# The chunk decay of units six to nine: two small DMAs from the last token's row instead of matmuls with a column of ones

## The chip, the cores and the metric

One core of one Trainium2 chip. The metric is device time in microseconds (us) of one execution, less being better; of the kernel before there are three timed runs, with a median of 182.37 us (182.37 to 183.64). One further execution was profiled; its trace is the source of all durations below.

## The reference

A gated linear attention runs over 768 tokens for 4 batches of 8 heads with 48 channels, and its output, laid out as 3072 tokens by 384 channels, goes through a two-layer perceptron with 2048 hidden units.

```python
f = 1.0 / (1.0 + np.exp(-f_logit))
for t in range(S):
    state = f[:, :, t, :, None] * state + np.einsum('bhd,bhe->bhde', k[:, :, t], v[:, :, t])
    y[:, :, t] = np.einsum('bhd,bhde->bhe', q[:, :, t], state)
...
h = x @ w_in
g = np.maximum(0.01 * h, h)
return (g @ w_out).astype(np.float32)
```

Inputs and output are float32.

## The kernel before

**Tiling.** The tokens are cut into six chunks of 128. A unit j is one chunk c of two batches, so there are twelve units, in the order c = 0 to 5 and, inside a chunk, two pairs of batches h. The half a (0 or 1) of a unit is one of its two batches. Tokens lie on the 128 partitions when data come in. With a running sum of log-decays inside a chunk, the recurrence becomes three matmul products per chunk (scores, masked scores by values, queries by the carried state), and a state that is carried from chunk to chunk.

**Steps of a unit, by their names in the order string.** `Lf`, `Lk`, `Lq`, `Lv` load a half of f, k, q, v (192 KB each, L100). `gate` (ScalarE, L140 and L141) turns f into lf = log(1 + exp(-f)), which is minus the log of the decay. `cs` (TensorE) sums lf over the tokens with an upper triangular matrix of ones (L146, 384 columns), so that row t of its PSUM tile holds the sum up to token t; row 127 is the whole chunk's. For all units but the last two (j below 10, where there is a next chunk), four more matmuls (L149) take lf itself as weights, two heads at a time, and multiply them by a column of ones: the sum over all tokens then comes out with head and channel on the partitions, four columns, in the same PSUM tile. `dec` (ScalarE) takes exponents: em and a from the 384 columns (L156, L157), and from those four columns the chunk's decay a_end (L160). `k` and `q` scale k and q; `v` casts v. For units 6 and up GpSimd does these, and `xk`, `xq` are DMA transposes on the SP queue (L203). `sc`, `mk`, `mx`, `xt` compute and copy out the unit's attention output. `pt` and `sf` compute and add the chunk's contribution to the state; `sb` (GpSimd, `state_end`) multiplies the state by a_end, a per-partition factor for each of four head pairs (L273), and casts it to bf16 (L276). `up`, `pr`, `dn`, `ob`, `st` are the perceptron: first layer (L293, L306), leaky relu on ScalarE (L299, L323), second layer (L328), copy out of PSUM, store (L341). `up` tiles go through two PSUM buffers (`ps_m`), so an `up` waits for the `pr` of the `up` two before it.

**Layout of the decay.** The state has 128 partitions: head i of a pair p has its 48 channels d at partitions 64 i to 64 i + 47, and the pair p is a column. The decay must come in that layout. In row 127 of the cs tile the same sums lie along one partition, as 384 columns (p, i, d).

**Order of the work.** All instructions are issued by one hand-written list, `order`; each engine runs its part of it in order. The SP queue issues all input loads, stores and DMA transposes, in the order of the list. Input tiles have six buffers for each of f, k, q, v, so the f tile of unit j is loaded anew by unit j + 6; for j from 6 on there is no such unit.

**Around the change.** In the list, loads run some two units ahead. The loads of unit 9's second half, for instance, follow `Lv_9_0` and stand shortly before `xq_8`; `gate_9` needs both halves of f of unit 9.

Of the kernel before, what the change touches and what calls it, by code (L numbers as in the profile page):

```python
# [9 lines left out]
FP32 = mybir.dt.float32  # L10
BF16 = mybir.dt.bfloat16
AF = mybir.ActivationFunctionType
# [3 lines left out]
def kernel(  # L16
# [10 lines left out]
    nc = tc.nc  # L27

    B, H, S, D = q.shape
    assert (B, H, S, D) == (4, 8, 768, 48)  # L30
    C = 128
    NCH = S // C
    P2 = H // 2
# [4 lines left out]
    pairs = [(c, h) for c in range(NCH) for h in range(B // 2)]  # L38
    NP = len(pairs)
    BY_UNIT = 6  # L40
    K_DVE = 6
    Q_DVE = 3
    CQ_ACT = 2

    const = ctx.enter_context(tc.tile_pool(name="const", bufs=1))
    inp = ctx.enter_context(tc.tile_pool(name="inp", bufs=6))
    work = ctx.enter_context(tc.tile_pool(name="work", bufs=2))
# [31 lines left out]
    w_in_b = [const.tile([128, NK, hi - lo], BF16, name="w_in_b", tag=f"w_in{lo}") for lo, hi in w_in_cols]  # L79
    w_out_b = const.tile([128, NF, KD], BF16, tag="w_out")  # L80

    for t in v2s:
        nc.gpsimd.memset(t[:, :, 1:3, :], 0.0)
    for t in state_b + state_f:
# [2 lines left out]
    st = {j: {} for j in range(NP)}  # L87
    srcs = {"f": f_logit, "k": k, "q": q, "v": v}

    def once(j, key, make):  # L90
        if key not in st[j]:
            st[j][key] = make()
        return st[j][key]

    def raw(j, name):
        return once(j, name + "_raw", lambda: inp.tile([128, 2, H, D], FP32, name=f"{name}_raw", tag=f"{name}_raw"))

    def load(j, name, a):
        c, h = pairs[j]
        nc.sync.dma_start(out=raw(j, name)[:, a],  # L100
                          in_=srcs[name][2 * h + a, :, c * C:(c + 1) * C, :].rearrange("h t d -> t h d"))
# [32 lines left out]
    def half(j, i):  # L134
        return slice(i, i + 1) if j < BY_UNIT else slice(0, 2)
# [7 lines left out]
    def cs(j, a):  # L143
        lf = lfs[j % NR]
        t = st[j]["cs", a] = ps_g.tile([128, 512], FP32, name="cs", tag="g")
        nc.tensor.matmul(t[:, 0:H * D], ut, lf[:, a, :, 0:D], start=True, stop=True)  # L146
        if pairs[j][0] < NCH - 1:
            for p in range(P2):
                nc.tensor.matmul(t[:, H * D + p:H * D + p + 1], lf[:, a, 2 * p:2 * p + 2, :], ones_col,  # L149
                                 start=True, stop=True)  # L150

    def dec(j, a):
        t = st[j].pop(("cs", a))
        em = once(j, "em", lambda: work.tile([128, 2, H * D], BF16, name="em_t", tag="em_t", bufs=3))
        at = once(j, "a", lambda: work.tile([128, 2, H * D], BF16, name="a_t", tag="a_t", bufs=3))
        nc.scalar.activation(em[:, a], t[:, 0:H * D], AF.Exp, scale=1.0)  # L156
        nc.scalar.activation(at[:, a], t[:, 0:H * D], AF.Exp, scale=-1.0)  # L157
        if pairs[j][0] < NCH - 1:
            end = st[j]["end", a] = work.tile([128, P2], FP32, name="a_end", tag="a_end", bufs=12)
            nc.scalar.activation(end, t[:, H * D:H * D + P2], AF.Exp, scale=-1.0)  # L160

    def scale_k(j, i):
        a = half(j, i)
# [4 lines left out]
    def scale_q(j, i):  # L168
        a = half(j, i)
        eng = nc.vector if j < Q_DVE else nc.gpsimd  # L170
        eng.tensor_mul(qhs[j % NR][:, a, :, 0:D], raw(j, "q")[:, a],  # L171
# [11 lines left out]
    def turned(j, x):  # L183
        return once(j, x + "T", lambda: work.tile([128, 2 * P2, 128], BF16, name=x + "T", tag=x + "T", bufs=3))
# [9 lines left out]
    def turn_out(j, a, x):  # L194
        out, src = turned(j, x)[:, P2 * a:P2 * a + P2, :], st[j].pop(("tp" + x, a))
        if x == "q" and j < CQ_ACT:
            nc.scalar.copy(out=out, in_=src)
# [160 lines left out]
    def store_part(j, a, i):  # L358
# [3 lines left out]

    parts = {
        "gate": gate, "cs": cs, "dec": dec, "k": scale_k, "q": scale_q, "v": cast_v,
        "tk": lambda j, a: turn(j, a, "k"), "tq": lambda j, a: turn(j, a, "q"),
        "ck": lambda j, a: turn_out(j, a, "k"), "cq": lambda j, a: turn_out(j, a, "q"),
        "xk": lambda j, a=None: turn_dma(j, "k", a), "xq": lambda j, a=None: turn_dma(j, "q", a),
        "sc": score, "mk": mask, "mx": mix, "xt": x_out, "pt": state, "sf": state_add, "sb": state_end,
        "up": up, "pr": relu, "uu": up_unit, "uh": up_half, "ph": relu_half, "pu": relu_unit, "W": weights, "H": hold, "dn": down, "ob": out_copy, "st": store,
        "dp": down_part, "op": out_part, "sp": store_part,  # L370
        "Lf": lambda j, a: load(j, "f", a), "Lk": lambda j, a: load(j, "k", a),
        "Lq": lambda j, a: load(j, "q", a), "Lv": lambda j, a: load(j, "v", a),
    }
# [27 lines left out]
    v_5_0 xt_4_1 tk_5_0 Lq_6_1 dec_5_1 dn_3_0_3 sb_3_1 dn_2_1_3 Lv_6_1 k_5_1 up_4_0 v_5_1 ob_2_1 Lf_7_0 pt_5_0 tq_5_0  # L401
    q_5_1 sf_5_0 dn_3_1_0 gate_6_0 st_2_1 up_4_1 ck_5_0 tk_5_1 Lk_7_0 dn_3_1_1 ck_5_1 pr_4_1 cq_5_0 tq_5_1 dn_3_1_2
    Lq_7_0 ob_3_0 pr_4_0 pt_5_1 Lv_7_0 cs_6_0 v_6_0 sf_5_1 dn_4_0_0 dec_6_0 cq_5_1 cs_6_1 st_3_0 up_4_2 sb_4_0 dec_6_1
    dn_3_1_3 Lf_7_1 up_4_3 pr_4_2 ob_3_1 k_6_0 Lk_7_1 sc_5_2 pr_4_3 up_4_4 st_3_1 mk_5_0_0 sb_4_1 dn_4_0_1 mk_5_1_0
    pr_4_4 xk_6 up_4_5 mk_5_0_1 q_6_0 pt_6_0 mk_5_1_1 up_4_6 pr_4_5 Lq_7_1 Lv_7_1 sf_6_0 gate_7_0 mx_5_2 up_4_7 xt_5_0
    sb_5_0 xq_6 pr_4_6 pt_6_1 xt_5_1 dn_4_0_2 pr_4_7 sf_6_1 up_5_0 Lf_8_0 cs_7_0 Lk_8_0 pr_5_0 up_5_1 dec_7_0 cs_7_1
    dn_4_0_3 Lq_8_0 up_5_2 pr_5_1 v_7_0 ob_4_0 dec_7_1 dn_4_1_0 Lv_8_0 up_5_3 sb_5_1 pr_5_2 st_4_0 dn_4_1_1 pr_5_3
    up_5_4 k_7_0 Lf_8_1 sc_6_2 pr_5_4 up_5_5 Lk_8_1 mk_6_0_1 q_7_0 dn_5_0_0 xk_7 mk_6_0_0 pr_5_5 up_5_6 mk_6_1_1
    dn_5_0_1 Lq_8_1 mk_6_1_0 pr_5_6 up_5_7 xq_7 mx_6_2 pr_5_7 gate_8_0 dn_4_1_2 Lv_8_1 xt_6_0 pt_7_0 xt_6_1 dn_5_0_2
    Lf_9_0 up_6_0 dn_5_0_3 pr_6_0 Lk_9_0 cs_8_0 ob_5_0 dn_4_1_3 dec_8_0 Lq_9_0 up_6_1 ob_4_1 cs_8_1 st_5_0 sf_7_0  # L410
    pr_6_1 up_6_2 dec_8_1 v_8_0 dn_6_0_0 st_4_1 up_6_3 pr_6_2 Lv_9_0 q_8_0 dn_5_1_0 pr_6_3 Lf_9_1 up_6_4 sc_7_2 Lk_9_1
    pr_6_4 k_8_0 up_6_5 mk_7_0_1 xq_8 dn_6_0_1 mk_7_0_0 pr_6_5 sb_6_0 up_6_6 mk_7_1_1 xk_8 dn_6_0_2 mk_7_1_0 pr_6_6
    sb_6_1 up_6_7 Lq_9_1 mx_7_2 pr_6_7 Lv_9_1 gate_9_0 dn_6_0_3 xt_7_0 sb_7_0 pt_7_1 pt_8_0 ob_6_0 dn_5_1_1 Lf_10_0
    sf_8_0 cs_9_0 dn_5_1_2 st_6_0 xt_7_1 dec_9_0 dn_6_1_0 sf_7_1 Lk_10_0 dn_5_1_3 dn_6_1_1 Lq_10_0 sc_8_2 Lv_10_0
    v_9_0 dn_6_1_2 mk_8_1_0 up_7_0 Lf_10_1 mk_8_1_1 sb_7_1 ob_5_1 up_7_1 pr_7_0 Lk_10_1 mk_8_0_1 dn_6_1_3 pr_7_1
    mk_8_0_0 st_5_1 up_7_2 cs_9_1 Lq_10_1 pr_7_2 up_7_3 dec_9_1 mx_8_2 Lv_10_1 up_7_4 pr_7_3 k_9_0 Lf_11_0 xt_8_0
    dn_7_0_0 xt_8_1 pr_7_4 Lk_11_0 ob_6_1 up_7_5 gate_10_0 sb_8_0 pt_9_0 xk_9 up_8_0 pt_9_1 q_9_0 dn_7_0_1 pr_7_5
    sf_9_1 st_6_1 pt_8_1 pr_8_0 cs_10_0 up_7_6 Lq_11_0 sf_8_1 dec_10_0 v_10_0 up_8_1 sf_9_0 pr_7_6 dn_7_0_2 xq_9
    sb_8_1 pr_8_1 cs_10_1 up_7_7 dec_10_1 up_8_2 Lv_11_0 Lf_11_1 pr_7_7 q_10_0 dn_8_0_0 pr_8_2 up_8_3 dn_7_0_3 Lk_11_1
    pr_8_3 k_10_0 up_8_4 ob_7_0 xq_10 dn_8_0_1 pr_8_4 dn_7_1_0 xk_10 up_8_5 sc_9_2 pr_8_5 st_7_0 up_8_6 mk_9_0_1  # L420
    gate_11_0 Lq_11_1 dn_7_1_1 mk_9_0_0 up_8_7 mk_9_1_0 pr_8_6 dn_7_1_2 mk_9_1_1 Lv_11_1 pr_8_7 dn_8_0_2 cs_11_0
    mx_9_2 dec_11_0 cs_11_1 xt_9_0 dn_7_1_3 dec_11_1 xt_9_1 dn_8_0_3 ob_7_1 k_11_0 up_9_0 ob_8_0 st_7_1 sc_10_2 pr_9_0
    st_8_0 dn_8_1_0 mk_10_1_0 q_11_0 xk_11 up_9_1 mk_10_0_0 dn_8_1_1 mk_10_1_1 pr_9_1 sb_9_0 up_9_2 xq_11 mk_10_0_1
    dn_9_0_0 pr_9_2 sb_9_1 up_9_3 mx_10_2 pr_9_3 v_11_0 up_9_4 xt_10_0 dn_9_0_1 xt_10_1 pr_9_4 up_9_5 up_10_0 pr_9_5
    sc_11_2 pr_10_0 up_10_1 mk_11_1_0 up_9_6 mk_11_0_0 pr_10_1 dn_9_0_2 mk_11_0_1 pr_9_6 up_10_2 mk_11_1_1 up_9_7
    pr_10_2 mx_11_2 pr_9_7 up_10_3 xt_11_0 dn_9_0_3 xt_11_1 pr_10_3 up_10_4 ob_9_0 up_11_0 st_9_0 pr_10_4 dn_8_1_2
    pr_11_0 up_10_5 up_11_1 pr_10_5 dn_8_1_3 pr_11_1 up_10_6 ob_8_1 up_11_2 st_8_1 pr_10_6 dn_9_1_0 pr_11_2 up_10_7
    up_11_3 pr_10_7 dn_9_1_1 pr_11_3 up_11_4 dn_9_1_2 pr_11_4 up_11_5 dn_9_1_3 pr_11_5 up_11_6 ob_9_1 dn_11_0_0
    st_9_1_2 pr_11_6 up_11_7 dn_10_0_0 pr_11_7 dn_11_0_1 dn_10_0_1 dn_11_0_2 dn_10_0_2 dn_11_0_3 dn_10_0_3 ob_11_0
    st_11_0_2 dn_11_1_0 ob_10_0 st_10_0 dn_11_1_1 dn_11_1_2 dn_11_1_3 dp_10_1_0 ob_11_1 st_11_1 op_10_1_0 sp_10_1_0  # L430
    dp_10_1_1 op_10_1_1 sp_10_1_1
    """
    for word in order.split():
        name, *numbers = word.split("_")
# [31 lines left out]
```

## Time and profile before

| | |
|---|---|
| Timed runs | 182.37, 183.64, 182.37 us |
| Profiled execution | 183.06 us, span on the core 181.3 us |
| TensorE busy | 168.4 us, 93% of the span |
| ScalarE, VectorE, GpSimd busy | 101.3, 88.1, 76.3 us |
| Matmuls of L149 | 80, of them 32 in units 6 to 9 (79.5 to 120.6 us) |
| a_end (L160) | 20 instructions, median 180 ns |
| Input loads | 96 of 192 KB, median 3.7 to 3.9 us from issue to landing |
| HBM traffic | 25.17 MB read, 4.72 MB written |

Starts are counted from the start of the span. [...] A load's row on the SP queue is the time that the queue takes to issue it, not its flight. The DMA share is the mean busy share of 16 DMA engines; it was 0.95 to 1.06 in every stretch from 20 to 147 us.

### The profile page before, as it was taken

Reading aid. Unit: us, or ns where it says so; the run is one execution under the profiler, and the core shown is the slowest. Engines: PE = TensorE matmul, PEld = TensorE weight load, DVE = VectorE, ACT = ScalarE, POOL = GpSimd, SP = SyncE. Lnnn points to the kernel's source line nnn. Section 1 sums busy time; section 2 is a strip of 40 time slices with the busy share of each in tenths; the row PEclk is TensorE's granted clock in tenths of the full one; section 3 lists DMA queues with packets and bytes.
Section 4 is the critical chain, followed back from the end, with each engine's and each line's share of the span. In section 5 each row is a group of like instructions: output and inputs, shape, how many; then the busy total and the mean of one; then the engine's idle time right before and its main releaser. Section 6 shows DMA issues by size and latency. Waiting matters only on the chain.

```text
span 181.3 us, 5431 instructions
## 1 busy us (share of the span) xinstructions
PE 168.4 (93%) x2264; PEld 131.4 (72%) x2264; DVE 88.1 (49%) x184; ACT 101.3 (56%) x207; POOL 76.3 (42%) x139
## 2 busy tenths in 40 slices
PE   0467999999999999999999999999999999999993
PEld 0245789776778888778877777688876788887663
DVE  2369750047778778657426425555135725311031
ACT  4475447456565757395865666268757346465100
POOL 8229900044754730939493186329730940000000
PEclk9999999999999999999999999999999999999999
DMA  6999999999998997899998999999996730110122
GB/s 121 194 217 192 188 209 215 193 186 251 200 214 173 213 219 156 169 228 254 161 240 165 213 214 189 209 231 187 219 172 161 120 88 4 43 47 0 43 87 87
DMA packets 118736, 30.23 MB, mean 167 GB/s; under 512 B 113080, under 2 KB 117944, under 8 KB 118712
## 3 DMA queue, kind: packets, MB, share of 16 engines
q1 hardware_dynamic: 116408, 26.75, 72.6%
q0 software_dynamic: 2304, 3.15, 10.1%
q8 instruction: 17, 0.28, 0.6%
q14 instruction: 7, 0.06, 0.1%
HBM read 25.17 MB, written 4.72 MB: 165 GB/s over the span
## 4 chain that ended last, share of the span: by engine, by line
PE 89%; SPq 6%; DMA 2%; ACT 1%; issue 0%; DVE 0%
PE po L328 34%; PE pm L293 24%; PE pm L306 12%; PE py L252 6%; SPq L100 6%; PE pw L219 4%; PE tp L192 3%; PE cs L146 2%; DMA f_raw<-in_f_logit_dram 2%; PE pt L263 2%; PE po L350 1%; PE pm L313 1%; PE cs L149 1%; ACT e_t L140 0%; ACT lf L141 0%
## 5 line engine op out<-in xcount | busy, mean ns | idle before, releaser
L328 PE MATMUL po<-w_out_b,gT 128*128 128x384 bf16 x368 | 71.6, 326 | 0.0
L299 ACT ACTIVATE gT<-pm 128x512 bf16<-128x512 f32 x64 | 37.8, 599 | 32.7 <-PE pm L293 32.3
L293 PE MATMUL pm<-xT,w_in_b 128*128 128x256 bf16 x384 | 51.0, 273 | 0.0
L328 PEld LDWEIGHTS <-gT 128*128 128x128 bf16 x368 | 33.8, 98 | 16.0 <-issue 0.2
L293 PEld LDWEIGHTS <-w_in_b 128*128 128x128 bf16 x384 | 40.0, 110 | 6.3
L224 DVE TENSOR_TENSOR wm<-pw,ut 128x512 bf16<-128x512 f32 x48 | 30.5, 684 | 17.6 <-PE pw L219 17.4
L333 DVE COPY osb<-po 128x384 f32<-128x384 f32 x23 | 12.8, 555 | 40.8 <-PE po L328 40.4
L178 POOL CAST v_b<-v_raw 128x384 bf16<-128x384 f32 (+1 forms) x18 | 11.1, 617 | 41.2 <-DMA v_raw<-in_v_dram 31.9
L323 ACT ACTIVATE gT<-pm 128x512 bf16<-128x512 f32 x30 | 17.9, 598 | 12.7 <-PE pm L306 11.9
L306 PE MATMUL pm<-xT,w_in_b 128*128 128x128 bf16 x360 | 24.2, 219 | 0.0
L306 PEld LDWEIGHTS <-w_in_b 128*128 128x128 bf16 x360 | 21.9, 110 | 1.7
L258 DVE CAST xT<-py 128x384 bf16<-128x384 f32 x24 | 12.7, 554 | 16.8 <-PE py L252 16.7
L171 POOL TENSOR_TENSOR qh<-q_raw,a_t 128x384 bf16<-128x384 f32 (+1 forms) x12 | 15.4, 1283 | 11.3 <-issue 6.0
L156 ACT ACTIVATE em_t<-cs 128x384 bf16<-128x384 f32 x24 | 11.8, 492 | 9.7 <-PE cs L149 8.0
L276 POOL CAST sb<-sf 64x192 bf16<-64x192 f32 x40 | 14.7, 367 | 2.5
L140 ACT ACTIVATE e_t<-f_raw 128x384 f32<-128x384 f32 (+1 forms) x18 | 11.3, 628 | 7.7 <-DMA f_raw<-in_f_logit_dram 7.7
L146 PE MATMUL cs<-lf,ut 128*128 128x384 bf16 x24 | 8.5, 353 | 6.7 <-ACT lf L141 6.7
L165 POOL TENSOR_TENSOR kh<-k_raw,em_t 128x768 bf16<-128x768 f32 x6 | 9.9, 1648 | 10.8 <-ACT em_t L156 7.4
L157 ACT ACTIVATE a_t<-cs 128x384 bf16<-128x384 f32 x24 | 11.8, 490 | 0.0
L141 ACT ACTIVATE lf<-e_t 128x384 bf16<-128x384 f32 (+1 forms) x18 | 11.3, 630 | 0.6
L273 POOL TENSOR_TENSOR sf<-sf,a_end 128x192 f32<-128x192 f32 x20 | 10.5, 524 | 2.2 <-DVE sf L269 1.8
L149 PEld LDWEIGHTS <-lf 128*128 128x128 bf16 x80 | 5.2, 100 | 7.6 <-issue 6.2
(51 smaller groups left out, 159.8 us busy)
## 6 DMA issues: line engine op xcount, KB each, us to landing
f_raw<-in_f_logit_dram SPq DMA_DIRECT2D x24, 192.0 KB, 3.9
k_raw<-in_k_dram SPq DMA_DIRECT2D x24, 192.0 KB, 3.8
q_raw<-in_q_dram SPq DMA_DIRECT2D x24, 192.0 KB, 3.7
v_raw<-in_v_dram SPq DMA_DIRECT2D x24, 192.0 KB, 3.7
out_dram<-osb SPq DMA_DIRECT2D x21, 192.0 KB, 3.0
w_out_b<-in_moe_w_out_dram POOLq DMA_DIRECT2D x4, 384.0 KB, 11.1
w_in_b<-in_moe_w_in_dram POOLq DMA_DIRECT2D x1, 768.0 KB, 10.0
w_in_b<-in_moe_w_in_dram POOLq DMA_DIRECT2D x2, 192.0 KB, 4.9
```

What stands on the lines that cost most here:

```text
L146: nc.tensor.matmul(t[:, 0:H * D], ut, lf[:, a, :, 0:D], start=True, stop=True)
L156: nc.scalar.activation(em[:, a], t[:, 0:H * D], AF.Exp, scale=1.0)
L171: eng.tensor_mul(qhs[j % NR][:, a, :, 0:D], raw(j, "q")[:, a], st[j]["a"][:, a].rearrange("t a (h d) -> t a h d", d=D))
L224: nc.vector.tensor_mul(wm, st[j].pop(("pw", a, i)), ut[:, None, :].to_broadcast([128, P2, 128]))
L258: nc.vector.tensor_copy(out=xT[:, :, a, :], in_=st[j].pop(("py", a))[:, 0:NK, :])
L276: nc.gpsimd.tensor_copy(out=sb[rows, a, :, i * D:i * D + D], in_=sf[rows, a])
L293: nc.tensor.matmul(pm[:, i, :], w_in(kk, ff), st[j]["xT"][:, kk].rearrange("t a s -> t (a s)"), start=(kk == 0), stop=(kk == NK - 1))
L299: nc.scalar.activation(gT[:, 2 * g:2 * g + 2, :], st[j].pop(("pm", g)), AF.Prelu, alpha=0.01)
L306: nc.tensor.matmul(pm[:, i, :], w_in(kk, ff), st[j]["xT"][:, kk, a, :], start=(kk == 0), stop=(kk == NK - 1))
L323: nc.scalar.activation(gT[:, 4 * g:4 * g + 4, 128 * a:128 * a + 128], st[j].pop(("pu", a, g)), AF.Prelu, alpha=0.01)
L328: nc.tensor.matmul(po, st[j]["g"][:, ff, 128 * a:128 * a + 128], w_out_b[:, ff, :], start=(ff == 0), stop=(ff == NF - 1))
L333: nc.vector.tensor_copy(out=osb, in_=st[j].pop(("po", a)))
```

## The change

For units 6 to 9 the 32 matmuls of L149 and the small exponent of L160 are taken out. In their place `dec` takes the exponent of the last 32 rows (partitions 96 to 127) of the cs tile, all 384 columns, and writes it as float32 into the unit's f tile, which is no longer needed; the columns are reordered as (i, d, a, p), so that the four p of one channel are neighbours (16 bytes) and the next channel stands 32 bytes further. Only row 127 is used; the two halves interleave in the tile. A new step `xe` then issues two DMAs on the SP queue, one for each head i: 1,536 bytes of partition 127 go to 48 partitions, 32 bytes each, in one of four constant tiles `end`, which GpSimd fills with ones at the start. `state_end` reads that tile. The step `xe_6` stands in the list after `Lk_7_1`, `xe_7` between `st_4_0` and `Lf_8_1`, `xe_8` between `Lv_9_0` and `Lf_9_1`, and `xe_9` between `Lf_11_0` and `Lk_11_0` of the SP queue's order. The rest of the list is the same.

```diff
+    END_DMA = 6
...
+    ends = [const.tile([128, 2, P2], FP32, name=f"end{i}", tag=f"end{i}") for i in range(4)]
+    for t in ends:
+        nc.gpsimd.memset(t, 1.0)
...
-        if pairs[j][0] < NCH - 1:
+        if pairs[j][0] < NCH - 1 and j < END_DMA:
             for p in range(P2):
                 nc.tensor.matmul(t[:, H * D + p:H * D + p + 1], lf[:, a, 2 * p:2 * p + 2, :], ones_col,
                                  start=True, stop=True)
...
         if pairs[j][0] < NCH - 1:
-            end = st[j]["end", a] = work.tile([128, P2], FP32, name="a_end", tag="a_end", bufs=12)
-            nc.scalar.activation(end, t[:, H * D:H * D + P2], AF.Exp, scale=-1.0)
+            if END_DMA <= j:
+
+                last = last_row(j)[96:128, :, :, a, :].rearrange("t i d p -> t p i d")
+                nc.scalar.activation(last, t[96:128, 0:H * D].rearrange("t (p i d) -> t p i d", p=P2, i=2), AF.Exp, scale=-1.0)
+                st[j]["end", a] = ends[j % 4][:, a]
+            else:
+                end = st[j]["end", a] = work.tile([128, P2], FP32, name="a_end", tag="a_end", bufs=12)
+                nc.scalar.activation(end, t[:, H * D:H * D + P2], AF.Exp, scale=-1.0)
+
+    def last_row(j):
+        return raw(j, "f").rearrange("t a h d -> t (a h d)").rearrange("t (i d a p) -> t i d a p", i=2, d=D, a=2)
+
+    def end_out(j):
+        last = raw(j, "f").rearrange("t a h d -> t (a h d)")[127:128]
+        for i in range(2):
+            nc.sync.dma_start(out=ends[j % 4][64 * i:64 * i + D].rearrange("d a p -> d (a p)"),
+                              in_=last[:, i * D * 2 * P2:(i + 1) * D * 2 * P2])
...
+        "xe": end_out,
```

More of the change, by code (lines that the diff above doesn't have):

```diff
@@ L369 @@
         "up": up, "pr": relu, "uu": up_unit, "uh": up_half, "ph": relu_half, "pu": relu_unit, "W": weights, "H": hold, "dn": down, "ob": out_copy, "st": store,
-        "dp": down_part, "op": out_part, "sp": store_part,
+        "xe": end_out, "dp": down_part, "op": out_part, "sp": store_part,
         "Lf": lambda j, a: load(j, "f", a), "Lk": lambda j, a: load(j, "k", a),
@@ L403 @@
     Lq_7_0 ob_3_0 pr_4_0 pt_5_1 Lv_7_0 cs_6_0 v_6_0 sf_5_1 dn_4_0_0 dec_6_0 cq_5_1 cs_6_1 st_3_0 up_4_2 sb_4_0 dec_6_1
[L404 to L431, printed above, removed]
+    dn_3_1_3 Lf_7_1 up_4_3 pr_4_2 ob_3_1 k_6_0 Lk_7_1 xe_6 sc_5_2 pr_4_3 up_4_4 st_3_1 mk_5_0_0 sb_4_1 dn_4_0_1
+    mk_5_1_0 pr_4_4 xk_6 up_4_5 mk_5_0_1 q_6_0 pt_6_0 mk_5_1_1 up_4_6 pr_4_5 Lq_7_1 Lv_7_1 sf_6_0 gate_7_0 mx_5_2
@@ new lines @@
+    up_4_7 xt_5_0 sb_5_0 xq_6 pr_4_6 pt_6_1 xt_5_1 dn_4_0_2 pr_4_7 sf_6_1 up_5_0 Lf_8_0 cs_7_0 Lk_8_0 pr_5_0 up_5_1
+    dec_7_0 cs_7_1 dn_4_0_3 Lq_8_0 up_5_2 pr_5_1 v_7_0 ob_4_0 dec_7_1 dn_4_1_0 Lv_8_0 up_5_3 sb_5_1 pr_5_2 st_4_0
+    dn_4_1_1 xe_7 pr_5_3 up_5_4 k_7_0 Lf_8_1 sc_6_2 pr_5_4 up_5_5 Lk_8_1 mk_6_0_1 q_7_0 dn_5_0_0 xk_7 mk_6_0_0 pr_5_5
+    up_5_6 mk_6_1_1 dn_5_0_1 Lq_8_1 mk_6_1_0 pr_5_6 up_5_7 xq_7 mx_6_2 pr_5_7 gate_8_0 dn_4_1_2 Lv_8_1 xt_6_0 pt_7_0
+    xt_6_1 dn_5_0_2 Lf_9_0 up_6_0 dn_5_0_3 pr_6_0 Lk_9_0 cs_8_0 ob_5_0 dn_4_1_3 dec_8_0 Lq_9_0 up_6_1 ob_4_1 cs_8_1
@@ new lines @@
+    st_5_0 sf_7_0 pr_6_1 up_6_2 dec_8_1 v_8_0 dn_6_0_0 st_4_1 up_6_3 pr_6_2 Lv_9_0 q_8_0 xe_8 dn_5_1_0 pr_6_3 Lf_9_1
+    up_6_4 sc_7_2 Lk_9_1 pr_6_4 k_8_0 up_6_5 mk_7_0_1 xq_8 dn_6_0_1 mk_7_0_0 pr_6_5 sb_6_0 up_6_6 mk_7_1_1 xk_8
+    dn_6_0_2 mk_7_1_0 pr_6_6 sb_6_1 up_6_7 Lq_9_1 mx_7_2 pr_6_7 Lv_9_1 gate_9_0 dn_6_0_3 xt_7_0 sb_7_0 pt_7_1 pt_8_0
+    ob_6_0 dn_5_1_1 Lf_10_0 sf_8_0 cs_9_0 dn_5_1_2 st_6_0 xt_7_1 dec_9_0 dn_6_1_0 sf_7_1 Lk_10_0 dn_5_1_3 dn_6_1_1
+    Lq_10_0 sc_8_2 Lv_10_0 v_9_0 dn_6_1_2 mk_8_1_0 up_7_0 Lf_10_1 mk_8_1_1 sb_7_1 ob_5_1 up_7_1 pr_7_0 Lk_10_1
@@ new lines @@
+    mk_8_0_1 dn_6_1_3 pr_7_1 mk_8_0_0 st_5_1 up_7_2 cs_9_1 Lq_10_1 pr_7_2 up_7_3 dec_9_1 mx_8_2 Lv_10_1 up_7_4 pr_7_3
+    k_9_0 Lf_11_0 xt_8_0 xe_9 dn_7_0_0 xt_8_1 pr_7_4 Lk_11_0 ob_6_1 up_7_5 gate_10_0 sb_8_0 pt_9_0 xk_9 up_8_0 pt_9_1
+    q_9_0 dn_7_0_1 pr_7_5 sf_9_1 st_6_1 pt_8_1 pr_8_0 cs_10_0 up_7_6 Lq_11_0 sf_8_1 dec_10_0 v_10_0 up_8_1 sf_9_0
+    pr_7_6 dn_7_0_2 xq_9 sb_8_1 pr_8_1 cs_10_1 up_7_7 dec_10_1 up_8_2 Lv_11_0 Lf_11_1 pr_7_7 q_10_0 dn_8_0_0 pr_8_2
+    up_8_3 dn_7_0_3 Lk_11_1 pr_8_3 k_10_0 up_8_4 ob_7_0 xq_10 dn_8_0_1 pr_8_4 dn_7_1_0 xk_10 up_8_5 sc_9_2 pr_8_5
@@ new lines @@
+    st_7_0 up_8_6 mk_9_0_1 gate_11_0 Lq_11_1 dn_7_1_1 mk_9_0_0 up_8_7 mk_9_1_0 pr_8_6 dn_7_1_2 mk_9_1_1 Lv_11_1 pr_8_7
+    dn_8_0_2 cs_11_0 mx_9_2 dec_11_0 cs_11_1 xt_9_0 dn_7_1_3 dec_11_1 xt_9_1 dn_8_0_3 ob_7_1 k_11_0 up_9_0 ob_8_0
+    st_7_1 sc_10_2 pr_9_0 st_8_0 dn_8_1_0 mk_10_1_0 q_11_0 xk_11 up_9_1 mk_10_0_0 dn_8_1_1 mk_10_1_1 pr_9_1 sb_9_0
+    up_9_2 xq_11 mk_10_0_1 dn_9_0_0 pr_9_2 sb_9_1 up_9_3 mx_10_2 pr_9_3 v_11_0 up_9_4 xt_10_0 dn_9_0_1 xt_10_1 pr_9_4
+    up_9_5 up_10_0 pr_9_5 sc_11_2 pr_10_0 up_10_1 mk_11_1_0 up_9_6 mk_11_0_0 pr_10_1 dn_9_0_2 mk_11_0_1 pr_9_6 up_10_2
@@ new lines @@
+    mk_11_1_1 up_9_7 pr_10_2 mx_11_2 pr_9_7 up_10_3 xt_11_0 dn_9_0_3 xt_11_1 pr_10_3 up_10_4 ob_9_0 up_11_0 st_9_0
+    pr_10_4 dn_8_1_2 pr_11_0 up_10_5 up_11_1 pr_10_5 dn_8_1_3 pr_11_1 up_10_6 ob_8_1 up_11_2 st_8_1 pr_10_6 dn_9_1_0
+    pr_11_2 up_10_7 up_11_3 pr_10_7 dn_9_1_1 pr_11_3 up_11_4 dn_9_1_2 pr_11_4 up_11_5 dn_9_1_3 pr_11_5 up_11_6 ob_9_1
+    dn_11_0_0 st_9_1_2 pr_11_6 up_11_7 dn_10_0_0 pr_11_7 dn_11_0_1 dn_10_0_1 dn_11_0_2 dn_10_0_2 dn_11_0_3 dn_10_0_3
+    ob_11_0 st_11_0_2 dn_11_1_0 ob_10_0 st_10_0 dn_11_1_1 dn_11_1_2 dn_11_1_3 dp_10_1_0 ob_11_1 st_11_1 op_10_1_0
@@ L432 @@
+    sp_10_1_0 dp_10_1_1 op_10_1_1 sp_10_1_1
     """
```

## The prediction

> **What bounds the kernel now.** I read the page first: how much each engine does, and the chain that ended last.
>
> ```profile
> PE 168.4 (93%) x2264; PEld 131.4 (72%) x2264; DVE 88.1 (49%) x184; ACT 101.3 (56%) x207; POOL 76.3 (42%) x139
> ...
> PE 89%; SPq 6%; DMA 2%; ACT 1%; issue 0%; DVE 0%
> ```
>
> TensorE is busy for 93% and makes up 89% of the chain; the rest is the start. But a busy TensorE may still be waiting inside its pipeline, so the second view is TensorE's own waits, over the whole span:
>
> ```profile
> PE cs L146 <- ACT lf L141: 6.7, 4, 4.7
> PE tp L192 <- DVE qh L171: 2.5, 2, 1.6
> PE pw L219 <- DVE kT L199: 0.6, 1, 0.6
> PE tp L192 <- DVE kh L165: 0.2, 1, 0.2
> ```
>
> The columns are total wait, times, longest. All ten microseconds lie in the start: asked from 45 us on, the same view is empty. From there to the last matmul the time is the sum of the start-to-start distances on TensorE, at a granted clock of 1.00. What leaves this stream shortens the kernel by its own distance, and what is added elsewhere costs nothing until it makes a matmul wait.
>
> **What the removed matmuls cost.** The third view is TensorE's timeline around two halves of unit 7 (first column start, second duration), then around a half of unit 10, which never had the matmuls of L149:
>
> ```profile
> 88.67 0.60 PE L293 MATMUL pm<-xT,w_in_b 128*128 128x256 bf16 x4
> 89.11 0.33 PE L146 MATMUL cs<-lf,ut 128*128 128x384 bf16 x1
> 89.27 0.24 PE L149 MATMUL cs<-ones_col,lf 128*128 128x1 bf16 x4
> 89.38 0.81 PE L293 MATMUL pm<-xT,w_in_b 128*128 128x256 bf16 x6
> 90.03 0.33 PE L146 MATMUL cs<-lf,ut 128*128 128x384 bf16 x1
> 90.19 0.24 PE L149 MATMUL cs<-ones_col,lf 128*128 128x1 bf16 x4
> 90.30 0.48 PE L328 MATMUL po<-w_out_b,gT 128*128 128x384 bf16 x2
> ...
> 128.25 0.33 PE L146 MATMUL cs<-lf,ut 128*128 128x384 bf16 x1
> 128.41 0.82 PE L293 MATMUL pm<-xT,w_in_b 128*128 128x256 bf16 x6
> ```
>
> From the start of L146 to the next matmul that is not L149 it is 89.38 - 89.11 = 0.27 us and 90.30 - 90.03 = 0.27, without L149 128.41 - 128.25 = 0.16. So four matmuls take 0.105 us, though each is recorded as 163 ns and their weight loads as 96 ns each. Of the other six halves of units 6 to 9, five show 0.26 to 0.27 and the first, at 79.31, shows 0.30. The sum: 8 x 0.105 and 0.03 for the first, less rounding, 0.85 us.
>
> **What is added, and what covers it.** ScalarE: in eight places an exponent of 32 x 384 with a scattered float32 output replaces one of 128 x 4.
>
> ```profile
> 80.14 0.49 ACT L157 ACTIVATE a_t<-cs 128x384 bf16<-128x384 f32 x1
> 80.51 0.18 ACT L160 ACTIVATE a_end<-cs 128x4 f32<-128x4 f32 x1
> 80.71 0.49 ACT L156 ACTIVATE em_t<-cs 128x384 bf16<-128x384 f32 x1
> 81.10 0.48 ACT L157 ACTIVATE a_t<-cs 128x384 bf16<-128x384 f32 x1
> 81.47 0.18 ACT L160 ACTIVATE a_end<-cs 128x4 f32<-128x4 f32 x1
> 81.52 0.62 ACT L299 ACTIVATE gT<-pm 128x512 bf16<-128x512 f32 x1
> ```
>
> The nearest row is L157, 0.49 us for 384 columns out of the same tile; the small one is 0.18. I take the difference, 0.31 us, for each half, 0.62 us for a unit (less in practice, since neighbours overlap); the bounds are nothing, if only the partitions used counted, and twice or three times the column time for the scattered output, which no row shows. Behind the second exponent the relu of L299 is queued, and for it waits the first-layer matmul two tiles on. That relu ends at 82.14 and TensorE takes its buffer at 83.15: 1.01 us of cover. In unit 7 the cover behind the two `dec` is 1.02 and 1.00 us; in unit 8 it is 0.76 us, but ScalarE idles 0.39 us between its two `dec`; in unit 9 it is 1.14 us. 0.62 us fits in all of them, so I cost it at nothing; uncovered it would be 4 x 0.62 = 2.5 us. em and a, which VectorE's and GpSimd's steps wait for, come 0.1 us earlier for the first half and at most 0.3 us later for the second; `kh` of unit 6 starts at 82.28 on a GpSimd that was busy until then, 1.1 us after its em.
>
> SP: `xe` adds two issues to each of four units. The SP timeline in front of unit 9's last f load:
>
> ```profile
> 103.15 2.52 SPq L341 DMA_DIRECT2D out_dram<-osb  x2
> 105.73 0.44 SPq L100 DMA_DIRECT2D v_raw<-in_v_dram  x1
> 106.22 0.70 SPq L100 DMA_DIRECT2D f_raw<-in_f_logit_dram  x1
> 106.96 0.75 SPq L100 DMA_DIRECT2D k_raw<-in_k_dram  x1
> 107.82 2.18 SPq L203 DMA_TRANSPOSE qT<-qh  x1
> ```
>
> No row shows a 48-piece DMA. The quickest issue of anything is a store at 0.33 us, a load takes 0.42 to about 1, a transpose up to 2.7. I take 0.4, near the store's, because the new DMAs have the fewest pieces: 0.8 us for a unit. `xe` waits for the second `dec` of its unit; in all four places that exponent ends before SP arrives (81.65 against 82.9 in unit 6, 105.1 against 106.2 in unit 8, with 0.31 us to add), so the wait itself holds up nothing. Behind `xe` are queued, in unit 6, a store and both transposes; in units 7 and 8 the load of f two units on; in unit 9 a load of k and a transpose. Who is waiting for these: the transposes of unit 6 are issued at 84.26 and 87.13, take about 4.5 us, and the scores start at 94.3, 2.5 us of cover; those of units 7 to 9 have 3 us or more. The closest load is the f half of unit 9 at 106.22. With the page's 3.9 us it lands at 110.1; `gate_9` starts at 111.67 only because the relu before it ends its stream then, ends at 113.37, and its `cs` starts at 113.61. The cover is 1.55 + 0.24 = 1.8 us. By then TensorE will be 0.65 us ahead, which leaves 1.15 us against six new issues in front of that load. Their 2.4 us do not add up in full: in this stretch SP repeatedly stands for other engines (two stores at 103.15 take 2.52 us where 0.33 each would do), so a delay is swallowed at such places. I cost this at nothing, and give it a rival.
>
> DMA engines: 116,408 packets fill 72.6% of 16 engines' 181.3 us, 18 ns each; 384 new pieces are 7 us of one engine, 0.4 us over 16. The decay is late for nobody: issued around 83, 93, 106 and 122.5 us and landed some 4 us later, it is read by L273 not before 108 (units 6 and 7), 123 and 143 us. The four fills on GpSimd take some 0.04 us each beside the fill of the ones column, and GpSimd then waits 1.8 us for its first v. The f tiles of units 6 to 9 are never loaded again, so no load waits for `xe`.
>
> The sum: the profiled execution of 183.06 us (span 181.3 and 1.8 around it) becomes 183.06 - 0.85 = 182.2. It lies 0.7 above the median of 182.37; scaled to that, the forecast is **181.5 us**, 0.47% less.
>
> **Rivals.** *Unit 9's gate is late (slower).* If SP absorbs nothing, six issues at 0.4 put the f load 2.4 us back: 2.4 - 1.15 = 1.25 us of stall at `cs_9`, net +0.4, 182.8 us. At 0.9 per issue it is 5.4 - 1.15 - 0.85 = +3.4, 185.8 us. The gain is lost once more than 2.0 us reach that load. For it: SP has hardly a gap, and the DMA share is 1.0 there. Against: the stores' long rows, and that a saturated DMA slows issues which the small DMAs need not pay for. Chance 0.09.
>
> *The scattered exponent is slow.* Written 32 bytes apart, it may take two column times more: 0.49 + 2 x 0.37 = 1.23 us. The extra is then about 0.9 and 1.05 us in a unit's two halves, 1.95 - 1.0 = 0.95 us of stall in unit 6 and in unit 7, 0.8 in unit 8, none in unit 9: 2.7 us, net +1.9, 184.2 us. With one column time more (0.86 us) the stalls are 0.2, 0.2 and 0.1, net -0.35, 182.0 us. No ScalarE row of this trace writes apart, so nothing in it excludes this. Chance 0.07, mostly for the milder. [...]
>
> *Nothing is gained,* because the ones matmuls hide behind weight loads that stay: 182.4 us. The 0.16 us distance without them speaks against it. Chance 0.04.
>
> **How the numbers follow.** The forecast has 0.80; it spans 180.8 to 182.2, by the 0.7 us between the profiled execution and the median. The range of 180.7 to 183.5 adds the mild forms of the rivals and leaves out both their harsh ends. Some 1% is what a measurement of this kernel can tell from no change (its three runs lie 0.7% apart). Faster by over 1% would need 1.8 us, twice what the stream holds of these matmuls: 0.06, for scatter. Slower by over 1% needs a harsh end of a rival, 2.7 us of new stalls: 0.10. Within 1%: 0.84.
>
> **What would show it.** Right: 48 matmuls of L149 left, 0.16 us from `cs` to the next matmul in units 6 to 9, TensorE's waits still empty from 45 us on, and span and matmul stream shorter by 0.85. A wait of L146 for ScalarE's lf near 113 us shows the first rival; an exponent of more than 0.9 us and L293 starting later behind it, the second. I am wrong if TensorE waits anywhere after the start.

## The result, and the profile after

The changed kernel took 184.43 us in the median of five runs (183.94 to 186.18), the kernel before, run beside it, 182.37 (182.13 to 183.64). The ratio is 1.0107, with a 95% interval of 1.0063 to 1.0151: slower by 1.1%, where 0.47% less was forecast. The profiled execution took 184.19 us, span 182.4.

The page's first lines, after:

```profile
PE 167.9 (92%) x2232; PEld 130.0 (71%) x2232; DVE 88.9 (49%) x184; ACT 108.1 (59%) x207; POOL 77.6 (43%) x143
...
PE 79%; ACT 6%; DMA 6%; SPq 3%; issue 2%; POOL 2%; DVE 0%; POOLq 0%
```

TensorE has its 32 matmuls less, but ScalarE is busy for 6.8 us more and stands for 6% of the chain, where it was 1%. TensorE's own waits from 45 us on, an empty view before:

```profile
PE pm L312 <- ACT gT L318: 1.5, 3, 0.8
PE pw L238 <- ACT f_raw L166: 0.5, 1, 0.5
```

Line numbers are 19 higher than before for the perceptron and the scores (L312 is the `up` of L293, L318 its relu, L238 the score), 4 for `cs` (L150); L166 is the new exponent. Both lines name ScalarE. Its timeline in unit 6, where the small exponents stood:

```profile
79.15 0.48 ACT L161 ACTIVATE a_t<-cs 128x384 bf16<-128x384 f32 x1
79.64 0.86 ACT L166 ACTIVATE f_raw<-cs 32x384 f32<-32x384 f32 x1
80.53 0.49 ACT L160 ACTIVATE em_t<-cs 128x384 bf16<-128x384 f32 x1
80.92 0.48 ACT L161 ACTIVATE a_t<-cs 128x384 bf16<-128x384 f32 x1
81.43 0.86 ACT L166 ACTIVATE f_raw<-cs 32x384 f32<-32x384 f32 x1
82.31 0.60 ACT L318 ACTIVATE gT<-pm 128x512 bf16<-128x512 f32 x1
```

From the start of a to the start of what follows the exponent it is 80.53 - 79.15 = 1.38 us and 82.31 - 80.92 = 1.39; before it was 80.71 - 80.14 = 0.57 and 81.52 - 81.10 = 0.42. A unit holds the relu up by 0.81 + 0.97 = 1.78 us more. TensorE at the same place:

```profile
81.43 0.45 PE L238 MATMUL pw<-qT,kT 48*128 48x128 bf16 x9
82.34 0.38 PE L238 MATMUL pw<-qT,kT 48*128 48x128 bf16 x7 [0.46 <-ACT f_raw L166]
82.96 0.49 PE L312 MATMUL pm<-xT,w_in_b 128*128 128x256 bf16 x3 [0.24 <-ACT gT L318]
```

The scores wait 0.46 us because the exponent still reads the cs tile whose PSUM buffer they need; then the first layer waits 0.24 us for the late relu. Unit 7 has one such wait of 0.80 us at the first layer, unit 8 one of 0.47, unit 9 none. Where nothing is late, the removal does what was forecast (unit 7, distances 0.17 and 0.16 instead of 0.27):

```profile
88.89 0.33 PE L150 MATMUL cs<-lf,ut 128*128 128x384 bf16 x1
89.06 0.82 PE L312 MATMUL pm<-xT,w_in_b 128*128 128x256 bf16 x6
89.71 0.33 PE L150 MATMUL cs<-lf,ut 128*128 128x384 bf16 x1
89.87 0.33 PE L347 MATMUL po<-w_out_b,gT 128*128 128x384 bf16 x1
```

Two measures are used below. The kernel's first 70 us differ from one execution to another (unit 5's first `cs` started between 69.5 and 73.3 us in the thirteen traces), so I take the **stretch** from unit 5's first `cs` to unit 10's first `cs`, which holds every edit: 55.44 us before (70.69 to 126.12), 57.50 after. That is 2.06 more, as is the difference of the medians, 184.43 - 182.37; that they agree so closely is chance, since the five runs alone spread over 2.2 us. With the 0.85 us of matmuls gone, 2.06 + 0.85 = 2.9 us of new waiting are in it. (The waits view shows 2.0 of them, because it counts from the modelled ends of matmuls, and a row reaches past the next start: `cs` above is 0.33 us long, and the next matmul starts 0.16 to 0.17 us after it. Its wait of 0.80 us in unit 7 is 1.13 us from start to start, where 0.16 is usual.)

The **short stretch** runs from unit 6's second `cs` to unit 10's first. It leaves out a wait that comes ahead of the exponents and DMAs of unit 6: the second-layer matmul behind unit 6's first `cs` needs a relu that is queued behind `gate_6`, and that gate needs its load. The distance from that `cs` to the next matmul was 0.16 to 0.98 us in the thirteen traces, and already 0.30 and 0.40 in the two of the kernel before. The short stretch holds seven of the eight halves, 7 x 0.105 = 0.73 us of the matmuls removed; it is 45.86 us before and 48.06 after. The trace of e3 below is of one of that kernel's two slow runs, so neither stretch is given for it.

### The profile page after: what moved, and what is told of

It reads as the page before. It is cut to its first block, busy times and chain, and to the rows that moved or that the text cites. A ratio compares the mean times of both kernels' runs of the same rounds, so it can differ in the third digit from the quotient of the medians.

```text
span 182.4 us, 5378 instructions
## 1 busy us (share of the span) xinstructions
PE 167.9 (92%) x2232; PEld 130.0 (71%) x2232; DVE 88.9 (49%) x184; ACT 108.1 (59%) x207; POOL 77.6 (43%) x143
## 4 chain that ended last, share of the span: by engine, by line
PE 79%; ACT 6%; DMA 6%; SPq 3%; issue 2%; POOL 2%; DVE 0%; POOLq 0%
PE po L347 31%; PE pm L312 22%; PE pm L325 12%; PE py L271 5%; DMA w_in_b<-in_moe_w_in_dram 4%; PE pw L238 3%; SPq L104 3%; ACT f_raw L166 2%; DMA v_raw<-in_v_dram 2%; PE tp L211 2%; PE cs L150 2%; ACT gT L318 2%; PE pt L282 1%; PE po L369 1%; ACT em_t L160 1%
## 5 line engine op out<-in xcount | busy, mean ns | idle before, releaser
L318 ACT ACTIVATE gT<-pm 128x512 bf16<-128x512 f32 x64 | 37.2, 596 | 29.5 <-PE pm L312 28.9
L312 PE MATMUL pm<-xT,w_in_b 128*128 128x256 bf16 x384 | 50.9, 273 | 1.5 <-ACT gT L318 1.5
L312 PEld LDWEIGHTS <-w_in_b 128*128 128x128 bf16 x384 | 40.3, 110 | 8.6 <-issue 2.1
L197 POOL CAST v_b<-v_raw 128x384 bf16<-128x384 f32 (+1 forms) x18 | 12.4, 690 | 41.2 <-DMA v_raw<-in_v_dram 41.1
L342 ACT ACTIVATE gT<-pm 128x512 bf16<-128x512 f32 x30 | 17.9, 598 | 12.3 <-PE pm L325 11.5
L160 ACT ACTIVATE em_t<-cs 128x384 bf16<-128x384 f32 x24 | 11.7, 489 | 9.7 <-PE cs L153 6.5
L150 PE MATMUL cs<-lf,ut 128*128 128x384 bf16 x24 | 8.5, 353 | 5.7 <-ACT lf L145 5.6
L238 PE MATMUL pw<-qT,kT 48*128 48x128 bf16 x192 | 9.0, 229 | 1.1 <-DVE kT L218 0.6
L287 DVE TENSOR_TENSOR sf<-sf,pt 64x192 f32<-64x192 f32 x20 | 6.8, 342 | 4.9 <-PE pt L282 2.0
```

The lines of the kernel that those rows point to most:

```text
L238: nc.tensor.matmul(st[j]["pw", a, i][:, p, :], kT[rows, P2 * a + p, :], qT[rows, P2 * a + p, :], start=True, stop=True)
L312: nc.tensor.matmul(pm[:, i, :], w_in(kk, ff), st[j]["xT"][:, kk].rearrange("t a s -> t (a s)"), start=(kk == 0), stop=(kk == NK - 1))
L318: nc.scalar.activation(gT[:, 2 * g:2 * g + 2, :], st[j].pop(("pm", g)), AF.Prelu, alpha=0.01)
L342: nc.scalar.activation(gT[:, 4 * g:4 * g + 4, 128 * a:128 * a + 128], st[j].pop(("pu", a, g)), AF.Prelu, alpha=0.01)
```

## The experiments

Theory A: the exponent's scattered output holds up ScalarE, and through it TensorE. Theory B: the DMAs' issues on SP make loads and transposes late. The kernels ran in three groups, each beside the kernel before; those runs had medians of 184.0, 183.37 and 183.02 us, so ratios and stretches are compared, not the absolute times of the expectations.

| kernel | exponent | DMAs | ratio, 95% interval | stretch, us | short stretch, us |
|---|---|---|---|---|---|
| before again | small | none | 0.9993 (0.9957 to 1.0030) | 55.55 | 45.86 |
| changed again | scattered | SP | 1.0120 (1.0065 to 1.0174) | 57.65 | 47.68 |
| e1 | scattered | none | 1.0108 (1.0056 to 1.0159) | 57.86 | 47.69 |
| e2, matmuls kept | small | SP | 1.0147 (1.0097 to 1.0197) | 57.30 | 47.42 |
| e3 | side by side | SP | 1.0192 (1.0126 to 1.0258) | - | - |
| e4 | none | none | 0.9976 (0.9938 to 1.0014) | 55.91 | 45.78 |
| e8 | side by side | none | 0.9963 (0.9928 to 0.9997) | 55.57 | 45.55 |
| e7 | VectorE copy | GpSimd | 0.9903 (0.9864 to 0.9943) | 55.34 | 45.12 |
| e7 again | VectorE copy | GpSimd | 0.9977 (0.9934 to 1.0020) | 54.82 | 45.25 |
| e10 | VectorE copy | SP | 1.0037 (1.0000 to 1.0074) | 55.17 | 45.73 |

**e1, no DMAs.** All `xe` steps are taken out of the list.

> Leaves out the eight DMAs (the state is multiplied by ones in units 6 to 9 instead of by the decay); the scattered exponents and the missing matmuls stay as changed. Theory A (the scattered exponents hold up the relus and the PSUM buffers, and so TensorE): about the changed kernel's time, 184.0 to 184.5 us, TensorE waiting some 2.5 to 3 us for ScalarE between 80 and 110 us. Theory B (the DMAs on the SP queue do the harm): 181.5 to 182 us.

The same ratio as the changed kernel, and the same first line in the waits view from 75 us on:

```profile
PE pm L312 <- ACT gT L318: 1.5, 3, 0.8
PE po L347 <- ACT gT L318: 0.6, 1, 0.6
```

So the exponent alone is enough for the whole loss, and in the changed kernel the DMAs add nothing to it that shows: the short stretch is 47.69 us here and 47.68 in the second trace of the changed kernel. The waits sum to 2.1 us in this view, less than the 2.5 to 3 expected; the second line is the relu behind `gate_6`.

**e2, the DMAs alone.**

```diff
-        if pairs[j][0] < NCH - 1 and j < END_DMA:
+        if pairs[j][0] < NCH - 1:
...
-            if END_DMA <= j:
+            if False:
```

> The kernel before with its matmuls of the ones column and its small exponents, plus the eight DMAs at the changed kernel's places; what they bring is not read, and they move f as loaded, without a wait for an exponent. Theory A: 182.4 us within 0.5, no TensorE wait after the start. Theory B: 184 us or more.

Theory A's expectation failed: with the DMAs alone the kernel is 1.5% slower. TensorE's waits in this kernel from 75 us on:

```profile
PE cs L150 <- DVE xT L277: 0.9, 1, 0.9
PE pw L238 <- DMA kT<-kh: 0.4, 1, 0.4
PE po L347 <- DVE sf L287: 0.2, 1, 0.2
```

The last one, at 81.26 us, comes ahead of the first small DMA at 84.85. SP's timeline, `xe_8` (L178) and unit 9's last f load behind it:

```profile
109.83 1.48 SPq L178 DMA_DIRECT2D end<-f_raw  x2
111.36 0.58 SPq L104 DMA_DIRECT2D f_raw<-in_f_logit_dram  x1
```

ScalarE's timeline at `gate_9`:

```profile
114.57 0.84 ACT L144 ACTIVATE e_t<-f_raw 128x768 f32<-128x768 f32 x1 [1.11 <-DMA f_raw<-in_f_logit_dram]
115.44 0.84 ACT L145 ACTIVATE lf<-e_t 128x768 bf16<-128x768 f32 x1
```

The gate waits 1.11 us for the load and ends at 116.28; `cs` of unit 9 starts at 116.33. The view names VectorE, but it is the late lf that ended this wait. The load is issued 111.36 - 103.61 = 7.75 us after unit 8's first `cs`, before 106.22 - 101.93 = 4.29. The 3.5 us between them look like six issues at their median of 0.586 us, but this distance varies too much for that: with no small DMA on SP at all it was 5.3 us in the second trace of the kernel before and 6.6 in e4. Counted from unit 5's first `cs`, the load is issued at 39.3 us here and at 39.1 and 39.0 in the two traces of the changed kernel, with six small issues ahead of it, and at 35.5 to 38.1 us in the eight traces with none. So they make it late, by some 1 to 4 us. In this trace the six held SP for 2.42 + 1.17 + 1.48 = 5.1 us; whether SP's long rows swallow a part of that is not settled.

The short stretch grows by 47.42 - 45.86 = 1.56 us, 0.9% of the kernel's time. The rest of the ratio lies ahead of the first of these DMAs, where this trace is 1.3 us behind that of before, and I did not settle whether that is chance.

**e3, the exponent side by side, DMAs as changed.**

```diff
-                last = last_row(j)[96:128, :, :, a, :].rearrange("t i d p -> t p i d")
+                last = raw(j, "f")[96:128, a].rearrange("t (p i) d -> t p i d", i=2)
```

> The changed kernel with the exponent's output written side by side instead of 32 bytes apart; the DMAs move the same bytes, which then stand in another order, so the decay is not the right one. If the scatter is what is slow (theory A1): the exponent takes 0.49 us instead of 0.87, TensorE's waits for ScalarE nearly vanish, 181.5 to 182.3 us. If 384 columns cost that much however they are written (A2): 0.8 us or more, and 184 us again.

The exponent fell to the length expected, and the kernel became no faster: 1.9% over the kernel before. Only lengths and kinds of wait are read from its trace. ScalarE's timeline in unit 6, one row:

```profile
83.17 0.48 ACT L166 ACTIVATE f_raw<-cs 32x384 f32<-32x384 f32 x1
```

TensorE's waits from 75 us on:

```profile
PE cs L150 <- ACT lf L145: 2.2, 2, 1.3
PE pw L238 <- DMA qT<-qh: 0.9, 1, 0.9
PE pm L312 <- ACT gT L318: 0.2, 1, 0.2
```

With the relus in time, TensorE runs into late lf, as in e2 (2.2 us in two waits), and into a late transpose (0.9 us). Against e8 below, the same kernel without the DMAs, the ratio is 1.0192 to 0.9963: here the DMAs cost some 2.3%. So the two costs hide one behind the other: with the scattered exponent the DMAs add nothing (e1), and with the exponent side by side they cost more than the scatter did.

**e4, neither exponent nor DMAs.** The two lines of the exponent and all `xe` steps are out.

> Leaves out the matmuls of the ones column and the exponents of units 6 to 9 and the DMAs too (the state is multiplied by ones). It measures the removed part by itself: by the forecast's first step 0.85 us less than before, 181.5 us (181.2 to 181.8), no TensorE wait after the start. If the matmuls had been hidden: 182.4 us.

The gain is not the 0.85 us expected: ratio 0.9976, an interval that holds both expectations. TensorE's waits from 75 us on:

```profile
PE po L345 <- ACT gT L316: 0.5, 1, 0.5
PE cs L150 <- ACT lf L145: 0.5, 1, 0.5
```

The first is the relu queued behind `gate_6`, the second is at `cs` of unit 9. Both gates start when their f load lands (the one of unit 9 at 112.86, landing 112.84). In this execution the cover of the loads was gone with nothing added to them. The short stretch is only 0.08 us under that of before; the second wait, 0.66 us more than usual from start to start, is the rest of the 0.73.

**The kernels before and after, once more.** They give a trace of each on the chip of e7 and e8.

> The kernel before, unchanged, so that its trace is of the same chip as the others of this group: ratio 1.000 within 0.4%. It shows how much cover the loads and relus of units 6 to 9 have on this chip, and whether TensorE waits at unit 9's cs there already.

> The changed kernel, unchanged: ratio 1.008 to 1.013 and the TensorE waits for ScalarE of some 2.5 to 3 us between 80 and 110 us again. If on this chip the waits lie elsewhere (at cs or pw, for loads and transposes), the DMAs share in the loss in this kernel too.

The first is as expected. So is the second in its ratio, but its waits for ScalarE come to 1.9 us in the view, not 2.5 to 3: 1.5 at the first layer and 0.4 for the relu behind `gate_6`. None is at `cs` or for a transpose, so the DMAs have no share that shows. In this trace of before, unit 9's f load lands at 110.91 and its gate starts at 111.40: 0.5 us of cover, where the first trace had 1.5.

**e8, side by side and no DMAs.** e3 with the `xe` steps out.

> The changed kernel without the DMAs and with the exponent written side by side (the state is multiplied by ones in units 6 to 9). With the scatter as ScalarE's whole trouble: exponent 0.49 us, TensorE waits for ScalarE under 0.5 us in total, ratio 0.994 to 1.000. If any 384-column exponent in that place is too long: ratio 1.005 or more.

The exponent and the ratio are as expected for the scatter; the waits for ScalarE, 0.6 us, are a little more than expected. TensorE's waits from 75 us on:

```profile
PE po L347 <- ACT gT L318: 0.4, 1, 0.4
PE pm L312 <- ACT gT L318: 0.2, 1, 0.2
```

The first is the relu behind `gate_6`, as in e4. The short stretch is 47.69 - 45.55 = 2.1 us shorter than e1's, from which this kernel differs by the order of the output alone. ScalarE's stream in unit 6, from the first em to the relu, takes 83.40 - 80.60 = 2.80 us here, 81.52 - 79.75 = 1.77 in the kernel before and 82.31 - 78.76 = 3.55 in the changed one. So two exponents side by side add 1.03 us to a unit, and their scatter 0.75 more.

**e7, another way to the same result.** No exponent is added; the DMAs leave SP.

```diff
+    def lay_out(j):
+        for a in range(2):
+            nc.vector.tensor_copy(out=last_row(j)[96:128, :, :, a, :].rearrange("t i d p -> t p i d"),
+                                  in_=st[j]["a"][96:128, a].rearrange("t (p i d) -> t p i d", p=P2, i=2))
...
-            nc.sync.dma_start(out=ends[j % 4][64 * i:64 * i + D].rearrange("d a p -> d (a p)"),
+            nc.gpsimd.dma_start(out=ends[j % 4][64 * i:64 * i + D].rearrange("d a p -> d (a p)"),
```

`le` (the copy) follows `xt` of the unit before; `xe_6` follows `q_7`, `xe_7` and `xe_8` precede `v_8` and `v_9`, `xe_9` follows `k_10`, where GpSimd idles (ahead of `v_8` for 6.72 us in the kernel before).

> Same result as the reference's, by another way: the exponent of the last row is not computed again; VectorE copies rows 96 to 127 of a, which hold it already, into the scattered order right after xt of the unit before, and GpSimd issues the two DMAs in its idle stretches, so ScalarE and SP have nothing added. If the two added costs (exponent on ScalarE, issues on SP) are the whole loss: 0.4% under before (ratio 0.993 to 0.999), no new TensorE wait. If a third thing costs (the small DMAs' traffic, the missing matmuls themselves): ratio above 1.003.

Faster than both kernels, but by more than the matmuls hold: the stretch is only 0.2 us shorter than that of before again (0.6 us went to the relu behind `gate_6`, the one wait in its view after 75 us), and 0.8 us lies in the first 70 us. The short stretch is 45.86 - 45.12 = 0.74 us shorter, what the matmuls in it hold. The ratio is outside what was expected, so I ran it again:

> The version with VectorE's copy and GpSimd's DMAs once more: ratio 0.988 to 0.997; between cs of unit 5 and cs of unit 10 no more than 55.4 us.

The ratio is just above what was expected, and its interval holds no change. The stretch is within it: TensorE waits nowhere after 75 us, and 55.55 - 54.82 = 0.73 us are gone, near the forecast's 0.85. The copy and the DMAs, from the view of the f tile in this run:

```profile
L175 DVE CAST f_raw<-a_t x8: 510/518/835, 87.8 to 123.1; 32x384 f32<-32x384 bf16 x8
L181 POOL DMA_DIRECT2D end<-f_raw x8: 504/518/568, 96.2 to 133.9; - x8
```

(columns after the count: min, median, max in ns, first and last start in us). VectorE writes the same scatter in 0.52 us; no run has it write side by side, so whether it pays for the distance is not shown.

**e10, the same on SP.** One word differs from e7, `nc.sync` for `nc.gpsimd`.

> The same version with its eight DMAs on the SP queue instead of GpSimd's, at the same places of the list (four issues stand ahead of unit 9's last f load). If SP swallows nothing: those four at 0.58 us put that load 2.3 us back, TensorE waits about 1 us at unit 9's cs, and the ratio is 0.4 to 0.8% above that of the version with GpSimd's DMAs. If the queue does not matter: the same ratio and no wait there.

The ratio is 0.6% above that of e7 run beside it, though the intervals of the two overlap. TensorE's waits from 75 us on are at `cs` of unit 9 and at a later score:

```profile
PE cs L150 <- ACT lf L145: 0.5, 1, 0.5
PE pw L241 <- DMA kT<-kh: 0.2, 1, 0.2
```

The wait at `cs` is half of what was expected, and it is no mark of the DMAs: e4 has the same wait without any, and the load was issued 37.3 us after unit 5's first `cs`, against 37.1 in e7's second trace. The wait for a transpose does bear on SP. Such waits after 75 us stand in e2, e3 and here, the kernels with small DMAs on SP and no scattered exponent, and in none of the eight traces without small DMAs on SP. Here it lies behind the stretch, and the part from unit 10's first `cs` to the end takes 55.6 us, against 55.2 in e7's two traces. The small DMAs' traffic is the same in e7 and here, so these numbers speak for the place on SP; a difference of 0.6% with overlapping intervals does not prove it.

**e9, what the distance costs.** The exponent writes into the f tile at four distances, 4, 8, 16, 32 bytes in units 6, 7, 8, 9, in passes where the tile is too short for one.

```diff
+                to = to[:, 0:H * D] if j == END_DMA else to.rearrange("t (c o s) -> t o c s", o=o, s=2)[:, :, :, 0]
```

> Only for the length of the exponent: as the changed kernel without its DMAs (ones in place of the decay), but units 6, 7, 8, 9 write the 384 values 4, 8, 16 and 32 bytes apart, the first half on 32 partitions, the second on all 128. [...] If only the large distance costs: 0.87 at 32 bytes alone.

ScalarE's timeline, its rows of this line (L173) and four that follow one:

```profile
82.20 0.48 ACT L173 ACTIVATE f_raw<-cs 32x384 f32<-32x384 f32 x1
82.71 0.49 ACT L160 ACTIVATE em_t<-cs 128x384 bf16<-128x384 f32 x1
...
83.47 0.50 ACT L173 ACTIVATE f_raw<-cs 128x384 f32<-128x384 f32 x1
83.84 1.22 ACT L325 ACTIVATE gT<-pm 128x512 bf16<-128x512 f32 x2
...
92.45 0.52 ACT L173 ACTIVATE f_raw<-cs 32x384 f32<-32x384 f32 x1
...
94.23 0.53 ACT L173 ACTIVATE f_raw<-cs 128x384 f32<-128x384 f32 x1
...
104.91 0.89 ACT L173 ACTIVATE f_raw<-cs 32x384 f32<-32x384 f32 x1
105.82 0.60 ACT L325 ACTIVATE gT<-pm 128x512 bf16<-128x512 f32 x1
...
107.06 0.89 ACT L173 ACTIVATE f_raw<-cs 128x384 f32<-128x384 f32 x1
107.70 1.16 ACT L325 ACTIVATE gT<-pm 128x512 bf16<-128x512 f32 x2
...
116.97 0.86 ACT L173 ACTIVATE f_raw<-cs 32x384 f32<-32x384 f32 x1
...
123.78 0.92 ACT L173 ACTIVATE f_raw<-cs 128x384 f32<-128x384 f32 x1
```

The step is between 8 and 16 bytes: 0.89 - 0.52 = 0.37 us on 384 values. At 16 bytes the exponent is as long as at 32, so it is not the large distance alone that costs; why the step lies there, no run shows. The number of partitions changes the recorded length by at most 0.06 us.

The starts show a second thing. Behind the exponent on 32 partitions (96 to 127) the next instruction starts 82.71 - 82.20 = 0.51 us later, or 105.82 - 104.91 = 0.91 at 16 bytes, more than its whole length. Behind the one on all 128 it is 83.84 - 83.47 = 0.37 and 107.70 - 107.06 = 0.64: these overlap with what follows, as L156 and L157 do in the kernel before (0.49 us long, with the next start 81.10 - 80.71 = 0.39 and 80.51 - 80.14 = 0.37 us after theirs). On 32 partitions the exponent is thus dearer for ScalarE's stream than on 128; whether their number or their place is the reason, no run shows.

## Why the prediction was wrong

- **The bound, and the removed matmuls: right.** The stream on TensorE sets the time, 0.16 us remain from `cs` to the next matmul, and e7's two traces show 0.74 and 0.61 us of the 0.73 that the short stretch holds.
- **The step that failed: "0.62 us fits in all of them, so I cost it at nothing".** The term was mis-sized: 0.31 us for a half was the difference of two durations, 0.49 and 0.18. ScalarE's stream grew by 0.81 and 0.97 us in unit 6, 1.78 us against some 1.0 of cover, and TensorE waited for it in units 6, 7 and 8. Two things were missed. The small exponent had hardly counted: the relu started 0.05 us after it, while the exponent on 32 partitions overlaps with neither neighbour (in unit 6 a's 0.48 us and its own 0.86 us are 0.49 to 0.51 and 0.88 to 0.89 us from start to start). Even side by side it adds 1.03 us to the unit (e8), not 0.62. And the scattered output took 0.86 to 0.88 us, not 0.49, which is 0.75 us more for the unit. The second is what made the loss: without it e8 is no slower than the kernel before.
- **The rival "the scattered exponent is slow" is what happened, with its price wrong.** Its milder form has the measured length, 0.86 us, but reckoned 1.95 - 2 x 0.37 = 1.2 us more for a unit, again from durations, and forecast 0.5 us of stalls; 1.78 came, and the stretch shows 2.9. That its harsh form gave 184.2 us, near the 184.43 measured, is luck: it supposed two column times more, 1.23 us for an exponent, which no run shows; at 32 bytes' distance the runs showed 0.86 to 0.92 us. The PSUM buffer that the exponent keeps from the scores was not seen at all: 0.46 us in unit 6 of this trace. Its chance of 0.07 was too low for a cost of which no row existed.
- **"I cost this at nothing" for SP fell as well,** though not in this kernel's time. An issue took 0.58 us in the median, not 0.4, and where the exponent was out of the way the DMAs cost 1.5% (e2) and some 2.3% (e3 against e8). In e2 `gate_9` waited 1.11 us for its load, and a score for a transpose that had been given 3 us of cover. How much SP's long rows swallow stays open. The wait of `xe` was costed at nothing, too; SP's waits in the changed kernel show 1 us of it, since `xe_8`'s second exponent ended at 107.06 and not near 105.4:

```profile
SPq L178 <- ACT f_raw L166: 1.0, 1, 1.0
```

- **The rival "unit 9's gate is late"** shows where the exponent is out of the way (e2, e3). In the changed kernel the load landed at 111.69, before the gate at 113.02, since ScalarE had stopped TensorE for some 2.9 us first.
- **The cover of the loads was read from one trace.** 1.5 us there, 0.5 in the second of the same kernel, none in e4 and in e7's second trace: a cover that hangs on a load was not a constant of the schedule.

## What to carry to other kernels

An instruction put in the place of another is to be costed by the distances between starts around the old one, not by the difference of durations: a short one may lie nearly wholly in its neighbours' overlap (here the relu started 0.05 us after an exponent of 0.18). Cost what no row shows at its bad end when several engines wait behind it, and look for the PSUM buffer it holds as well as for who is queued. Before trusting a cover that hangs on a load, read it from a second execution. Small DMAs on a queue without gaps can make what stands behind them late (a load by some 1 to 4 us in e2), so an engine with idle stretches is the place to try first; the runs here favour it without proving it.

## What the runs showed of the hardware

- ScalarE, 384 float32 values into SBUF (e9): 0.48 to 0.50 us at 4 bytes' distance, 0.52 to 0.53 at 8, 0.89 at 16, 0.86 to 0.92 at 32, on 32 partitions and on 128 alike. To the next start it is 0.51 us on partitions 96 to 127 and 0.37 on all 128, both at 4 bytes. VectorE's copy from bf16 at 32 bytes (e7): 0.52 us.
- A DMA of 48 pieces of 32 bytes holds SP for 0.58 us in the median (0.55 to 1.11 in the changed kernel), more than a 192 KB store at its quickest (0.33 us in the kernel before), and lands after 1.7 to 3.6 us. Issued by GpSimd it holds that queue for 0.50 to 0.57 us (e7).
- A store's issue on SP in the kernel before: 0.53 us in the median from 20 to 147 us, at a DMA share of 0.95 to 1.06, and 0.33 to 0.42 us after that, at a share of 0.12 (four of the last eight are of 96 KB, the rest of 192).
